# Float32 attention chunks: 1/sum moved from the weights of the values to their output, and every remainder of the MLP weights taken on VectorE

## Chip, cores and metric

One core of one Trainium2 chip runs the whole program. The metric is the device time of one execution in microseconds; lower is better. Engines are TensorE (PE in the rows: matmuls; PEld: its weight loads), VectorE (DVE), ScalarE (ACT), GpSimd (POOL) and SyncE (SP, which issues the transfers).

## What is computed

Sliding-window attention with sink tokens, then a two-layer MLP on its output:

```python
B, H, S, D = 4, 8, 768, 64          # n_sink = 4, window = 128
scores = q @ k.T / sqrt(D)           # keep: sink columns, or 0 <= row - col < window
scores = where(keep, scores, -1e9);  scores -= max(scores)
a = exp(scores);  a = a / (sum(a) + 1e-9)
x = (a @ v), heads side by side      # 3072 tokens x 512
h = x @ w_in;  r = max(h, 0)         # 512 x 2048
out = (s * r * r + b) @ w_out        # 2048 x 512
```

All inputs and the output are float32.

## The kernel before

**Chunks.** The 3072 tokens are eight chunks of 384 rows (three blocks of 128), taken in `ORDER`; for each chunk the attention of eight heads is made first, as four pairs of heads, and then the MLP reads it. Chunks 0 and 1 lie at the start of their sequences and use class `Plain`, with float32 matmuls; chunks 2 to 7 use `attn_slots`, which splits operands in two fp32r halves. Chunk 0's attention runs by itself. While the MLP of chunk c runs on TensorE, the slots of the attention of chunk c + 1 are woven in between its steps (the last loop of `tile_kernel`).

**The MLP.** `moe_steps` goes through 16 slices f of the hidden layer. `l1(f)` makes `h` with twelve matmuls (L608), then r (L611, ScalarE), s r r (L614, VectorE), g and its remainder (L616 ScalarE, L617 VectorE). `l2(f)`, two steps later, adds nine matmuls into three output banks `po` (L628). x, g and the weights each are a pair: a value rounded to fp32r and a remainder in fp32r; three products of a pair with a pair are taken. In chunk 0 (where `before` is set) s r r is written back into the PSUM bank of `h`, so this bank is held until L617 has read it. The banks of `h`, of the scores `sc`, of `o` and, in chunk 1, of the transposes `tp` come from one pool of five, `psA`.

**The weights.** They stay in SBUF as pairs, and are made once, while chunk 0 is computed. `load_weight(f)` brings slice f (1 MB) into the place of slice f + 1 as 64-bit numbers read as pairs of 32-bit words; `make_weight` turns it into float32 and then into the pair. `make_weight(2f)` has two ScalarE steps (L217, L218), two VectorE steps (L219, L220) and an addition on GpSimd in pieces of 256 columns (`in_parts`, L206). `make_weight(2f + 1)` writes the rounded value over place f (L226, ScalarE), and the following `make_weight(2f + 2)` the remainder: for even f on VectorE in one instruction (L231), for odd f on GpSimd in pieces (again L206). Slices 0 to 12 are one tile of 1024 columns, 13 and 14 are two pieces of 512, and 15 is four of 256. Since the raw slice f lies in the place of slice f + 1, L226 of f + 1 waits for the remainder of f.

**`Plain`.** For each pair: `scores` (matmuls L510, mask and maximum L525, exponential with row sum L527), `norm` (sum + 1e-9, reciprocal, and six scales of the weights of the values by it, L538), `turned` in three parts (transposes L550, copied out of PSUM by L552), `values` (matmuls L561; the rounded x by L563 on ScalarE, its remainder by L564 on VectorE).

**Order.** The program's text gives priorities; a scheduler sets the order on each engine, so that an edit can move neighbours. Each engine then runs its list strictly in order.

The lines of the weights that the change touches:

```python
        f -= 1
        if j % 2 == 0 and f >= 0:
            for c, raw in enumerate(raws[f]):
                do = in_parts if f % 2 == 1 else nc.vector.tensor_tensor
                do(out=piece(f, c, 1), in0=raw[..., 0].bitcast(F32), in1=piece(f, c, 0).bitcast(F32), op=ALU.subtract)
```

Of the kernel before, what the change touches and what calls it, by code (L numbers as in the profile page):

```python
# [6 lines left out]
F32 = mybir.dt.float32  # L7
# [5 lines left out]
ALU = mybir.AluOpType  # L13
AX = mybir.AxisListType

P = 128
B, H, S, D = 4, 8, 768, 64
ORDER = ((0, 0), (1, 0), (0, 1), (1, 1), (2, 0), (2, 1), (3, 0), (3, 1))
NS = 8
BLK = 3  # L20
CH = BLK * P
# [12 lines left out]
RB, VB = 1, 2  # L34
# [7 lines left out]
def tile_kernel(ctx, tc, qT, kT, k0, v, vsk, n_sink, window, w, s, b, out):  # L42
    nc = tc.nc
# [5 lines left out]
    def ps(name):  # L49
        return psA.tile([P, 512], F32, tag="a", name=name)  # L50

    wk_cm = tc.tile_pool(name="wk", bufs=2)
    wk = wk_cm.__enter__()
# [8 lines left out]
    ident = identr.bitcast(F32)  # L62
# [105 lines left out]
    def place(f):  # L168
        return (const if f < NEARLY else late[0]).tile([P, 2, 2, DM], F32, tag=f"w{f}", name=f"w{f}")
# [15 lines left out]
    def scratch(f, j):  # L185

        if len(raws[f]) == 1:
            tag = f"w{NF - 2 + f % 2}"
            return (late[0] if late else first).tile([P, 2, DM], I32, tag=tag, name="wt", bufs=1)
        return wk.tile([P, DM], I32, tag="ot", name="wt")[:, :raws[f][j].shape[1]]  # L190

    def piece(f, j, t):

        n = len(raws[f])
        if n == 1:
            return weight[f][:, :, t, :]
        a = DM * 2 // n
        return weight[f][:, j * 2 // n, t, j * a % DM:j * a % DM + a]

    def in_parts(out, in0, in1, op):  # L200

        n = out.shape[-1]
        for c in range(out.shape[1] if len(out.shape) == 3 else 1):
            for a in range(0, n, PART):
                q = (slice(None),) + ((c,) if len(out.shape) == 3 else ()) + (slice(a, min(a + PART, n)),)
                nc.gpsimd.tensor_tensor(out=out[q], in0=in0[q], in1=in1[q], op=op)  # L206

    def make_weight(j):

        f = j // 2
        if j % 2 == 0 and f < NF:
            for i, raw in enumerate(raws[f]):
                lo, hi = raw[..., 0], raw[..., 1]
                t = scratch(f, i)
                nc.scalar.activation(lo, lo.bitcast(U32), AF.Copy, scale=2.0 ** -29)  # L217
                nc.scalar.mul(hi.bitcast(F32), hi.bitcast(F32), 2.0 ** -111)  # L218
                nc.vector.tensor_scalar(out=t, in0=hi, scalar1=3, scalar2=None, op0=ALU.logical_shift_left)  # L219
                nc.vector.scalar_tensor_tensor(out=hi, in0=hi, scalar=-0x80000000, in1=t,  # L220
                                               op0=ALU.bitwise_and, op1=ALU.bitwise_or)
                in_parts(lo, hi, lo, ALU.add)
        if j % 2 == 1:
            weight[f] = place(f).bitcast(F32R)
            for c, raw in enumerate(raws[f]):
                nc.scalar.copy(piece(f, c, 0), raw[..., 1].bitcast(F32))  # L226
        f -= 1
        if j % 2 == 0 and f >= 0:
            for c, raw in enumerate(raws[f]):
                do = in_parts if f % 2 == 1 else nc.vector.tensor_tensor  # L230
                do(out=piece(f, c, 1), in0=raw[..., 0].bitcast(F32), in1=piece(f, c, 0).bitcast(F32), op=ALU.subtract)  # L231
            raws.pop(f)


# [227 lines left out]
    class Plain:  # L462
# [66 lines left out]
        def norm(self, pr):  # L529

            pp = self.pairs[pr]
            nc.vector.tensor_scalar(out=pp.z[:, 1], in0=pp.z[:, 0], scalar1=1e-9, scalar2=None, op0=ALU.add)
            nc.vector.reciprocal(out=pp.z[:, 0], in_=pp.z[:, 1])
            for i in range(BLK):
                c0, n = (0, P, 0)[i], (i + 1) * P
                for hh in range(2):
                    sm = pp.sm[2 * (i // 2) + hh][:, c0:c0 + n]
                    nc.vector.tensor_scalar(out=sm, in0=sm, scalar1=pp.z[:, 0, i, hh:hh + 1], scalar2=None, op0=ALU.mult)  # L538

        def turned(self, pr, part):  # L540

            pp = self.pairs[pr]
            if part == 0:
                pp.t = (wk if self.c else first).tile([P, 2, 2 * BLK, P], F32, tag="hl" if self.c else "tt0", name="tf", bufs=2)
            tp = (ps if self.c else po_bank)("tp")
            pos = (((0, 0), (2, 2)), ((1, 0), (1, 1)), ((2, 0), (2, 1)))[part]
            for hh in range(2):
                for j, (i, kb) in enumerate(pos):
                    c0 = (0, P, 0)[i] + kb * P
                    nc.tensor.transpose(tp[:, (2 * hh + j) * P:(2 * hh + j + 1) * P], pp.sm[2 * (i // 2) + hh][:, c0:c0 + P], ident)  # L550
            out = pp.t[:, :, part:part + (6 if part == 0 else 3):(5 if part == 0 else 2)]
            nc.scalar.copy(out, tp.rearrange("p (h k c) -> p h k c", h=2, c=P))  # L552

        def values(self, pr):
            pp = self.pairs.pop(pr)
            o = ps("o")
            for kb in range(BLK):
                for hh in range(2):
                    a = (0, 3, 5)[kb]
                    hs = slice(hh * D, (hh + 1) * D)  # L560
                    nc.tensor.matmul(o[hs, kb * P:CH], pp.v[:, kb, hh], pp.t[:, hh, a:a + BLK - kb].rearrange("p k c -> p (k c)"),  # L561
                                     start=(kb == 0), stop=(kb == BLK - 1))
            nc.scalar.copy(self.x[0][:, pr, :], o[:, :CH])  # L563
            nc.vector.tensor_tensor(out=self.x[1][:, pr, :], in0=o[:, :CH], in1=self.x[0][:, pr, :].bitcast(F32), op=ALU.subtract)  # L564

    def po_bank(name):
        return psO.tile([P, 512], F32, tag="po", name=name)
# [29 lines left out]
    def moe_steps(x, store, wk, before=None, last=False):  # L597
        g = {}
        po = [None] * BLK

        def l1(f):
            if before:
                before(f)
            h = ps("h")
            i = 0
            for cc in range(NCC):
                for wi, xi in ((0, 0), (0, 1), (1, 0)):
                    nc.tensor.matmul(h[:, :CH], weight[f][:, 0, wi, cc * P:(cc + 1) * P], x[xi][:, cc, :], start=(i == 0), stop=(i == 11))  # L608
                    i += 1
            r = wk.tile([P, CH], F32, tag="xsk" if before and f % 2 else "r", name="r", bufs=RB)  # L610
            nc.scalar.activation(r, h[:, :CH], AF.Relu, scale=1.0 / WUP)  # L611

            hr = h[:, :CH] if before else r
            nc.vector.scalar_tensor_tensor(out=hr, in0=h[:, :CH], scalar=sw_ap, in1=r, op0=ALU.mult, op1=ALU.mult)  # L614
            gg = wk.tile([P, 2, CH], F32R, tag="g", name="g", bufs=3)
            nc.scalar.activation(gg[:, 0, :], hr, AF.Identity, bias=b_ap, scale=1.0)  # L616
            nc.vector.scalar_tensor_tensor(out=gg[:, 1, :], in0=hr, scalar=b_ap, in1=gg[:, 0, :].bitcast(F32),  # L617
                                           op0=ALU.add, op1=ALU.subtract)
            g[f] = gg

        def l2(f):
            gg = g.pop(f)
            for tb in range(BLK):
                if f == 0:
                    po[tb] = psO.tile([P, DM], F32, tag="po", name="po")
                tsl = slice(tb * P, (tb + 1) * P)
                for i, (gi, wi) in enumerate(((0, 0), (0, 1), (1, 0))):
                    nc.tensor.matmul(po[tb], gg[:, gi, tsl], weight[f][:, 1, wi, :],  # L628
                                     start=(f == 0 and i == 0), stop=(f == NF - 1 and i == 2))
                if f == NF - 1:  # L630
                    own = dict(tag="kh", bufs=2) if tb == 2 else dict(tag="hl", bufs=HLB)
                    ot = wk.tile([P, DM], F32, name="ot", **(own if last else dict(tag="ot")))
                    nc.scalar.mul(ot, po[tb], 1.0 / WUP)
                    store(tb, ot)

        steps = []
        for f in range(NF + L2):
            if f < NF:
                steps.append(lambda f=f: l1(f))
            if f >= L2:  # L640
                steps.append(lambda f=f: l2(f - L2))
        return steps
# [101 lines left out]
    def before(f):  # L744
        weights(f + 2 + LOADS // 2, 2 * f + 5)
# [17 lines left out]
    k, slots = plain_slots(0)  # L763
# [19 lines left out]
    for c in range(NC_):  # L783
# [5 lines left out]
        if c + 1 < NC_:  # L789
            k, slots = plain_slots(1) if c == 0 else attn_slots(c + 1)  # L790
        i = 0
# [56 lines left out]
```

## Time and profile before

| | us |
|---|---|
| three runs | 730.23, 731.99, 732.29 |
| median | 731.99 |
| the profiled execution | 733.05 |
| its span, first to last instruction | 731.3 |
| chunk 0's attention, until the first L608 | 44.5 |
| first pass through the weights (MLP of chunk 0), until the next chunk's L608 | 44.5 to 150.8 |

Mean granted clock of TensorE over the span: 0.977 of full speed. The trace gives for each instruction its engine, line, operands, start and duration, and what ended the idle time before it. "x12" stands for twelve merged instructions; each float32 matmul of L510 and L561 is recorded as two. Durations of neighbours on an engine overlap by some tenths of a microsecond, so that a sum of single durations is a little more than the busy time.

### The profile page before, as it was taken

The numbers are of one execution on the slowest core, as the hardware profiler recorded it, in microseconds if no ns is written. First come the engines' busy times: TensorE is split into PE (matmuls) and PEld (weight loads), VectorE is DVE, ScalarE is ACT, GpSimd is POOL, SyncE is SP. The second block draws the span as 40 slices with busy tenths as digits, with TensorE's granted clock in tenths as the row PEclk, the third lists the DMA queues.
The fourth block names the chain that finished last, engine by engine and source line by source line (L and its number), as shares of the span: only waits on it lengthen the run. The fifth ranks groups of instructions, "written<-read, shape, count | busy, mean of one in ns | idle before, by whom it ended". The sixth has DMA issues, their size and how long they took to land.

```text
span 731.3 us, 11917 instructions
## 1 busy us (share of the span) xinstructions
PE 700.8 (96%) x3812; PEld 617.5 (84%) x3812; DVE 508.2 (69%) x1202; ACT 473.5 (65%) x1157; POOL 410.8 (56%) x703
## 2 busy tenths in 40 slices
PE   7599898999999999999999999999999999999996
PEld 4267666889988999899998999899999999989895
DVE  6969988548985788657786588847787589743331
ACT  6978877467774687656784677747775577633222
POOL 2556886348892588716674488915765389810000
PEclk8889988999999999999999999999999999999999
DMA  7845031131210212111111222111111212000001
GB/s 289 333 173 216 12 137 37 52 103 48 89 56 24 90 56 63 34 62 54 45 58 49 75 70 63 45 51 51 57 52 56 72 42 69 3 19 26 0 1 48
DMA packets 27381, 52.62 MB, mean 72 GB/s; under 512 B 3504, under 2 KB 15536, under 8 KB 25392
## 3 DMA queue, kind: packets, MB, share of 16 engines
q1 hardware_dynamic: 27312, 51.79, 21.3%
q8 instruction: 32, 0.52, 0.3%
q14 instruction: 37, 0.30, 0.1%
HBM read 45.49 MB, written 6.29 MB: 71 GB/s over the span
## 4 chain that ended last, share of the span: by engine, by line
PE 78%; DVE 9%; POOL 7%; ACT 3%; issue 2%; DMA 0%; SPq 0%; POOLq 0%; ACTq 0%; DVEq 0%
PE h L608 32%; PE po L628 32%; POOL w L206 4%; PE o L383 3%; PE sc L309 2%; PE sc L310 2%; PE sc L330 2%; DVE w L220 1%; PE tp L550 1%; PE o L561 1%; DVE smf L538 1%; DVE wt L219 1%; PE o L375 1%; POOL hl L346 1%; POOL kl L290 1%
## 5 line engine op out<-in xcount | busy, mean ns | idle before, releaser
L608 PE MATMUL h<-x,w 128*128 128x384 f32 x1536 | 297.7, 343 | 6.7 <-ACT tf L552 3.4
L628 PE MATMUL po<-w,g 128*128 128x512 f32 x1152 | 299.1, 405 | 0.0
L608 PEld LDWEIGHTS h<-x,w 128*128 128x128 f32 x1536 | 266.4, 189 | 13.1 <-ACT tf L552 3.8
L628 PEld LDWEIGHTS po<-w,g 128*128 128x128 f32 x1152 | 211.9, 191 | 45.6 <-issue 2.1
L614 DVE SCALAR_TENSOR_TENSOR r<-h,sb,r 128x384 f32<-128x384 f32 x112 | 68.9, 615 | 78.8 <-ACT r L611 77.7
L611 ACT ACTIVATE r<-h 128x384 f32<-128x384 f32 x128 | 62.6, 489 | 91.8 <-PE h L608 82.6
L617 DVE SCALAR_TENSOR_TENSOR g<-r,sb,g 128x384 fp32r<-128x384 f32 x112 | 91.1, 814 | 31.1 <-ACT g L616 29.6
L346 POOL TENSOR_TENSOR hl<-two,hl 128x256 fp32r<-128x256 f32 x128 | 102.3, 800 | 15.5 <-ACT hl L345 12.9
L323 POOL TENSOR_TENSOR sm<-sm 128x128 f32<-128x128 f32 x128 | 67.3, 526 | 60.9 <-ACT sm L320 59.1
L320 ACT ACTIVATE sm<-sm,negm 128x264 f32<-128x264 f32 (+1 forms) x144 | 72.1, 501 | 28.6 <-DVE negm L314 27.3
L616 ACT ACTIVATE g<-r,sb 128x384 fp32r<-128x384 f32 x112 | 69.1, 617 | 22.7 <-DVE r L614 22.0
L290 POOL TENSOR_TENSOR kl<-kraw,kh 128x528 fp32r<-128x528 f32 (+1 forms) x48 | 60.3, 1257 | 19.1 <-ACT kh L288 18.8
L206 POOL TENSOR_TENSOR w<-w 128x256 int32<-128x256 int32 x60 | 45.0, 780 | 40.3 <-DVE w L220 32.0
L345 ACT CAST hl<-two 128x256 fp32r<-128x256 f32 x128 | 50.5, 395 | 25.8 <-DVE two L343 25.5
L343 DVE TENSOR_TENSOR two<-sc,split 128x256 f32<-128x256 f32 x128 | 53.1, 417 | 5.8 <-POOL hl L346 5.5
L324 POOL COPY psk<-sm 128x24 f32<-128x24 f32 x144 | 35.5, 246 | 17.1 <-ACT sm L320 17.0
L383 PE MATMUL o<-hl,vv 128*128 128x256 f32 (+1 forms) x256 | 44.3, 275 | 0.0
L383 PEld LDWEIGHTS o<-hl,vv 128*128 128x128 f32 x256 | 39.6, 188 | 3.2
L289 DVE TENSOR_TENSOR qs<-qraw,qs 64x384 fp32r<-64x384 f32 x48 | 39.6, 825 | 3.7 <-ACT qs L285 1.9
L314 DVE CUSTOM_DVE_ANT_0 sm<-sc,m_all 128x264 f32<-128x264 f32 x64 | 27.3, 426 | 21.2 <-PE sc L310 19.2
L314 DVE CUSTOM_DVE_ANT_0 sm<-sc,msk 128x264 f32<-128x264 f32 (+1 forms) x80 | 32.0, 400 | 14.1 <-PE sc L310 13.4
L309 PE MATMUL sc<-kh,qs 128*128 128x264 f32 (+1 forms) x144 | 41.6, 291 | 0.0
(138 smaller groups left out, 960.4 us busy)
## 6 DMA issues: line engine op xcount, KB each, us to landing
w<-in_w SPq DMA_DIRECT2D x15, 1024.0 KB, 8.8
kraw<-in_kT SPq DMA_DIRECT2D x32, 264.0 KB, 2.6
out<-ot SPq DMA_DIRECT2D x24, 256.0 KB, 2.0
qraw<-in_qT SPq DMA_DIRECT2D x24, 192.0 KB, 2.4
vraw<-in_v SPq DMA_DIRECT2D x16, 256.0 KB, 2.8
kraw<-in_kT SPq DMA_DIRECT2D x16, 200.0 KB, 2.5
vsraw<-in_vsk SPq DMA_DIRECT2D x24, 64.0 KB, 2.1
vraw<-in_v SPq DMA_DIRECT2D x8, 192.0 KB, 2.4
```

What stands on the lines that cost most here:

```text
L206: nc.gpsimd.tensor_tensor(out=out[q], in0=in0[q], in1=in1[q], op=op)
L290: nc.gpsimd.tensor_tensor(out=hd.kl[:, :kw], in0=hd.k[:, :kw], in1=hd.kh[:, :kw].bitcast(F32), op=ALU.subtract)
L320: nc.scalar.activation(sm[:, :n], sm[:, :n], AF.Exp, bias=negm[:, uu], scale=-1.0, accum_out=pp.zz[:, i, hh:hh + 1])
L323: nc.gpsimd.tensor_tensor(out=sm[:, c1:c1 + P], in0=sm[:, p1:p1 + P], in1=sm[:, c1:c1 + P], op=ALU.add)
L346: nc.gpsimd.tensor_tensor(out=lo, in0=both, in1=hi.bitcast(F32), op=ALU.subtract)
L383: nc.tensor.matmul(hd.o[:, q0:q0 + n * P], hd.vv[:, kb, :], hd.hl[:, t, c0 * P:(c0 + n) * P], start=(hd.n == 0), stop=(i == BLK - 1 and kb ...
L608: nc.tensor.matmul(h[:, :CH], weight[f][:, 0, wi, cc * P:(cc + 1) * P], x[xi][:, cc, :], start=(i == 0), stop=(i == 11))
L611: nc.scalar.activation(r, h[:, :CH], AF.Relu, scale=1.0 / WUP)
L614: nc.vector.scalar_tensor_tensor(out=hr, in0=h[:, :CH], scalar=sw_ap, in1=r, op0=ALU.mult, op1=ALU.mult)
L616: nc.scalar.activation(gg[:, 0, :], hr, AF.Identity, bias=b_ap, scale=1.0)
L617: nc.vector.scalar_tensor_tensor(out=gg[:, 1, :], in0=hr, scalar=b_ap, in1=gg[:, 0, :].bitcast(F32), op0=ALU.add, op1=ALU.subtract)
L628: nc.tensor.matmul(po[tb], gg[:, gi, tsl], weight[f][:, 1, wi, :], start=(f == 0 and i == 0), stop=(f == NF - 1 and i == 2))
```

## The change

Four edits:
- `make_weight`: the remainder of odd f is taken on VectorE too, in whole pieces.
- `norm`: the six scales of each pair go; the reciprocal stays.
- `values`: six matmuls with the identity spread the reciprocals over the 64 output partitions of each head, into a bank `zb`. VectorE copies `o` to SBUF, multiplies it by `zb`, and the rounded x and its remainder are taken from the product. The product's tile has the tag "xsk" with one buffer; r in odd steps of chunk 0 had that tag, and has "r" now.
- `turned`: in chunk 0 the copy of part 1 moves from ScalarE to VectorE.

```diff
@@ make_weight
-                do = in_parts if f % 2 == 1 else nc.vector.tensor_tensor
-                do(out=piece(f, c, 1), in0=raw[..., 0].bitcast(F32), in1=piece(f, c, 0).bitcast(F32), op=ALU.subtract)
+                nc.vector.tensor_tensor(out=piece(f, c, 1), in0=raw[..., 0].bitcast(F32), in1=piece(f, c, 0).bitcast(F32), op=ALU.subtract)
@@ norm
-            for i in range(BLK):
-                c0, n = (0, P, 0)[i], (i + 1) * P
-                for hh in range(2):
-                    sm = pp.sm[2 * (i // 2) + hh][:, c0:c0 + n]
-                    nc.vector.tensor_scalar(out=sm, in0=sm, scalar1=pp.z[:, 0, i, hh:hh + 1], scalar2=None, op0=ALU.mult)
@@ turned
-            nc.scalar.copy(out, tp.rearrange("p (h k c) -> p h k c", h=2, c=P))
+            (nc.vector.tensor_copy if self.c == 0 and part == 1 else nc.scalar.copy)(out, tp.rearrange("p (h k c) -> p h k c", h=2, c=P))
@@ values
-            nc.scalar.copy(self.x[0][:, pr, :], o[:, :CH])
-            nc.vector.tensor_tensor(out=self.x[1][:, pr, :], in0=o[:, :CH], in1=self.x[0][:, pr, :].bitcast(F32), op=ALU.subtract)
+            zb = (ps if self.c else po_bank)("zb")
+            for i in range(BLK):
+                for hh in range(2):
+                    nc.tensor.matmul(zb[hh * D:(hh + 1) * D, i * P:(i + 1) * P], pp.z[:, 0, i, hh:hh + 1].to_broadcast([P, D]), ident,
+                                     start=True, stop=True)
+            y = wk.tile([P, CH], F32, tag="xsk", name="y0", bufs=1)
+            nc.vector.tensor_copy(y, o[:, :CH])
+            nc.vector.tensor_tensor(out=y, in0=zb[:, :CH], in1=y, op=ALU.mult)
+            nc.scalar.copy(self.x[0][:, pr, :], y)
+            nc.vector.tensor_tensor(out=self.x[1][:, pr, :], in0=y, in1=self.x[0][:, pr, :].bitcast(F32), op=ALU.subtract)
@@ l1
-            r = wk.tile([P, CH], F32, tag="xsk" if before and f % 2 else "r", name="r", bufs=RB)
+            r = wk.tile([P, CH], F32, tag="r", name="r", bufs=RB)
```

Line numbers shift: L614, L616 and L617 are L616, L618 and L619 after the change, L231 is L230, L608 is L610.

What the scheduler makes of it on GpSimd, at the weights f = 10 to 13 (the number in a tile's name is only its serial number; `w_824<-w_824` is the addition, `w_1070<-w_824,w_1070` the remainder, both L206). Before:

```order
L206 TENSOR_TENSOR w_749<-w_749 128x256 x4
L206 TENSOR_TENSOR w_824<-w_824 128x256 x4
L206 TENSOR_TENSOR w_1070<-w_824,w_1070 128x256 x4
L206 TENSOR_TENSOR w_895<-w_895 128x256 x4
L206 TENSOR_TENSOR w_1085<-w_1085 128x256 x2
L206 TENSOR_TENSOR w_1209<-w_1085,w_1209 128x256 x2
L206 TENSOR_TENSOR w_1085<-w_1085 128x256 x2
L206 TENSOR_TENSOR w_1209<-w_1085,w_1209 128x256 x2
```

Now:

```order
L206 TENSOR_TENSOR w_708<-w_708 128x256 x4
L206 TENSOR_TENSOR w_750<-w_750 128x256 x4
L206 TENSOR_TENSOR w_816<-w_816 128x256 x4
L206 TENSOR_TENSOR w_887<-w_887 128x256 x4
L206 TENSOR_TENSOR w_1075<-w_1075 128x256 x4
```

The remainders are gone from this list; only the additions are left.

On VectorE, at the weight f = 12 (`wt` and `w` in L219 and L220 are its two steps). Before:

```order
L220 SCALAR_TENSOR_TENSOR w_895<-w_895,wt 128x1024
L532 TENSOR_SCALAR zf<-zf 128x6
L533 RECIPROCAL zf<-zf 128x6
L538 TENSOR_SCALAR smf<-smf,zf 128x128 x2
L538 TENSOR_SCALAR smf<-smf,zf 128x256 x2
L538 TENSOR_SCALAR smf<-smf,zf 128x384
L538 TENSOR_SCALAR psk_96<-psk_96,zf 128x384
L231 TENSOR_TENSOR w_1134<-w_895,w_1134 128x2x512
L614 SCALAR_TENSOR_TENSOR h<-h,sb,r 128x384
L617 SCALAR_TENSOR_TENSOR g<-h,sb,g 128x384
```

Now:

```order
L220 SCALAR_TENSOR_TENSOR w_887<-w_887,wt 128x1024
L616 SCALAR_TENSOR_TENSOR h<-h,sb,r 128x384
L563 COPY y_1120<-o 128x384
L230 TENSOR_TENSOR w_1134<-w_887,w_1134 128x2x512
L619 SCALAR_TENSOR_TENSOR g<-h,sb,g 128x384
L564 TENSOR_TENSOR y_1120<-zb,y_1120 128x384
L566 TENSOR_TENSOR x_1_497<-y_1120,x_1_496 128x384
L219 TENSOR_SCALAR wt<-w_1075 128x512
```

The six scales are gone; the remainder, which reads what GpSimd adds after L220, now stands three places behind L220, with L619 behind it, and the copy and the product of the values have come in.

On TensorE, at a pair of values in chunk 1. Now:

```order
L555 MATMUL o<-tf,vf 64x384 x2
L555 MATMUL o<-tf,vf 64x256 x2
L555 MATMUL o<-tf,vf 64x128 x2
L560 MATMUL zb<-identr,zf 64x128 x6
L630 MATMUL po<-w_875,g 128x512 x9
```

The six matmuls of `zb` stand between the values and the next nine of `po`; the rest of the list keeps its sequence there, and from the MLP of chunk 1 on it is the same as before.

## Rows read from the trace of the kernel before

**Rows 1.** The page, part 4: chain that ended last, shares by line.

```profile
PE h L608 32%; PE po L628 32%; POOL w L206 4%; PE o L383 3%; PE sc L309 2%; PE sc L310 2%; PE sc L330 2%; DVE w L220 1%; PE tp L550 1%; PE o L561 1%; DVE smf L538 1%; DVE wt L219 1%; PE o L375 1%; POOL hl L346 1%; POOL kl L290 1%
```

**Rows 2.** Windows by stage: start:end, length, busy by engine (count), PEclk, DMA share, GB/s.

```profile
5.00:44.50 39.50, 27.08 (x149) 16.19 (x147) 33.42 (x119) 31.84 (x75) 13.95 (x21) 0.78 0.71 282
44.50:93.00 48.50, 43.60 (x226) 34.20 (x224) 44.10 (x85) 40.63 (x75) 36.92 (x44) 1.00 0.39 151
93.00:124.00 31.00, 27.75 (x119) 20.81 (x120) 25.15 (x49) 24.22 (x52) 22.57 (x29) 0.83 0.29 103
124.00:151.00 27.00, 27.00 (x141) 22.48 (x140) 14.81 (x30) 13.56 (x30) 9.00 (x13) 0.94 0.15 45
151.00:731.00 580.00, 571.54 (x3174) 522.34 (x3172) 389.77 (x917) 361.59 (x926) 325.69 (x584) 1.00 0.17 51
```

**Rows 3.** Waits of TensorE, 0 to 140 us: us, times, longest.

```profile
PE tp L550 <- DVE sm L538: 7.4, 2, 5.2
...
PE sc L510 <- DVE g L617: 3.4, 3, 2.2
PE h L608 <- ACT tf L552: 3.4, 2, 2.2
PE h L608 <- DVE g L617: 1.4, 1, 1.4
```

**Rows 4.** Waits of all engines, 0 to 135 us.

```profile
ACT w L226 <- POOL w L206: 9.0, 5, 3.7
...
DVE w L231 <- POOL w L206: 5.0, 3, 3.3
```

**Rows 5.** Timeline: start, us, engine, line, tiles [idle before <-releaser].

```profile
105.35 2.35 PE L608 MATMUL h<-x,w 128*128 128x384 f32 x12
...
115.68 0.91 PE L510 MATMUL sc<-kf,qf 64*128 64x384 f32 x2 [0.88 <-DVE g L617]
...
119.93 1.93 POOL L206 TENSOR_TENSOR w<-w,w 128x256 fp32r<-128x256 f32 x2
...
121.83 2.32 POOL L206 TENSOR_TENSOR w<-w 128x256 int32<-128x256 int32 x4
121.90 0.66 ACT L226 CAST w<-w 128x512 fp32r<-128x512 f32 x1 [3.72 <-POOL w L206]
...
122.45 0.60 ACT L552 COPY tf<-tp 128x512 f32<-128x512 f32 x1
...
123.10 3.56 PE L608 MATMUL h<-x,w 128*128 128x384 f32 x12 [2.22 <-ACT tf L552]
```

**Rows 6.** Busy time of L538 alone, by stage.

```profile
5.00:44.50 39.50, 9.74 (x24) 0.78 0.71 282
44.50:151.00 106.50, 14.44 (x24) 0.94 0.30 110
```

**Rows 7.** Groups by line, 0 to 130 us: us busy, mean ns.

```profile
L206 POOL TENSOR_TENSOR w<-w 128x256 int32<-128x256 int32 x60 | 45.0, 780 | 40.3 <-DVE w L220 32.0 <-ACT w L218 8.3
L206 POOL TENSOR_TENSOR w<-w,w 128x256 fp32r<-128x256 f32 x28 | 27.9, 1025 | 2.7 <-ACT w L226 2.7
...
L231 DVE TENSOR_TENSOR w<-w,w 128x1024 fp32r<-128x1024 f32 x7 | 9.4, 1346 | 5.0 <-POOL w L206 5.0
...
L552 ACT COPY tf<-tp 128x512 f32<-128x512 f32 x21 | 12.0, 580 | 1.1 <-PE tp L550 0.9
```

**Rows 8.** Single lines, min/median/max ns.

```profile
L231 DVE TENSOR_TENSOR w<-w,w x9: 676/1214/1619, 29.3 to 131.5; 128x1024 fp32r<-128x1024 f32 x7, 128x512 fp32r<-128x512 f32 x2
...
L564 DVE TENSOR_TENSOR x<-o,x x8: 546/555/559, 19.1 to 149.2; 128x384 fp32r<-128x384 f32 x8
```

**Rows 9.** Timeline of TensorE at the last pair of chunk 1.

```profile
147.12 1.51 PE L561 MATMUL o<-tf,vf 128*64 128x384 f32 x12
148.56 2.36 PE L628 MATMUL po<-w,g 128*128 128x512 f32 x9
```

**Rows 10.** Timeline: end of chunk 0's attention.

```profile
46.56 0.55 DVE L564 TENSOR_TENSOR x<-o,x 128x384 fp32r<-128x384 f32 x1
```

## The prediction

> **What bounds the kernel now.** The chain that ended last is mostly two matmul lines of TensorE, L608 and L628, with GpSimd's L206 as the largest entry of another engine [rows 1]. The windows by stage show where that entry lies [rows 2]. From 151 us on TensorE is busy 571.5 of 580 us at full clock: nothing the other engines save there counts. Before that there are two stages with slack. In the attention of chunk 0 (5 to 44.5 us) TensorE works 27.1 of 39.5 us at a granted clock of 0.78, while VectorE is busy 33.4 and ScalarE 31.8. In the first pass through the weights (44.5 to 151 us) TensorE idles in short gaps and its clock falls: 0.83 from 93 to 124 us and 0.94 from 124 to 151, that is, part of the time at 1.2 instead of 2.4 GHz.
>
> The waits of TensorE name these gaps [rows 3]: 7.4 us for the scales of L538, all in the first stage; in the second 3.4 us and 1.4 us for L617 and 3.4 us for L552, 8.2 us in all. The waits of the others say who stands behind them [rows 4]: ScalarE's L226 waits 9.0 us for GpSimd, VectorE's L231 5.0 us. One place shows the whole chain [rows 5]: GpSimd subtracts a remainder until 121.86, ScalarE has idled 3.72 us in front of L226, which needs it, the copy L552 queued behind L226 runs at 122.45, and TensorE, idle 2.22 us for that copy, starts its matmuls at 123.10, at half clock: 3.56 us for the twelve, which took 2.35 at 105.35 us [rows 5].
>
> So the limit of the second stage is the making of weights and the queues it runs through. Its slack: 8.2 us idle, and for the clock 0.17 x 2 x 31 + 0.06 x 2 x 27 = 13.8 us at 1.2 GHz, of which 3.1 us (the 0.88 and 2.22 us gaps in it [rows 5]) are idle and counted already; the remaining 10.7 us of work would have taken 5.3 us less. Slack: 13.5 us of 106.5.
>
> **The change part by part.** *Scales out.* The 48 instructions of L538 go: 9.7 us of VectorE in the first stage, 14.4 us in the second [rows 6]. The transposes no longer wait for them; they wait for the exponentials alone.
>
> *Remainders to VectorE.* GpSimd loses 32 pieces at about 1.02 us [rows 7], an estimated 32 us; all but the four of f = 1, some 28 us, lie in the second stage. VectorE gains six of 1024 columns, two of 512 and four of 256. The wide one exists in the trace, 1.35 us on average, between 1.21 and 1.62 [rows 7, 8]; the small ones are bounded by 0.68 (the shortest of L231, which has 512 columns [rows 8]) and half of that. That is 1.35 in the first stage (f = 1), and 5 x 1.35 + 2 x 0.68 + 4 x 0.35 = 9.5 us in the second. The spread from 1.21 to 1.62 is what the rows show when GpSimd works beside it. The Trainium skill (GPSIMD Engine Reference, Key points) says why: GpSimd shares its SBUF interfaces with VectorE, and instructions with two SBUF inputs contend. By that rule, which speaks against moving a two-input subtract, every wide one would cost 1.62, and VectorE would pay 1.4 us more in the second stage. I keep 1.35, because GpSimd's own load there falls by these 28 of 68.5 us [rows 2].
>
> *Product behind the values.* Each of eight pairs adds a copy and a multiply of 384 columns that read PSUM. The nearest row is L564, of that size and also reading PSUM, 0.55 us [rows 8]: 1.1 us a pair, 4.4 us in each stage. The subtract is there before and after, and so is ScalarE's copy.
>
> *Copies.* In chunk 0 four copies of 512 columns leave ScalarE, 4 x 0.58 = 2.3 us [rows 7], for VectorE, taken at 0.65 each between 0.55 (L564) and 0.74 (L564 by columns): 2.6 us.
>
> *TensorE.* Six small matmuls a pair (zb), 768 columns. The nearest rows are the value matmuls, also float32 with 64-wide weights: 1536 columns in 1.44 us to the start of the next group, recorded as twelve [rows 9]. By columns that is 0.72 us a pair, by number of records 1.44, as each float32 matmul there shows as two. I take 0.72, since the form is the same: 2.9 us in the second stage; 5.8 is the upper end. In the first stage they lie in idle time. The Trainium skill (FP8 and Floating Point Precision, TensorE Precision Notes) says that true FP32 takes four passes through the array; by 4 x 768 columns at 2.4 GHz that would be an estimated 1.28 us a pair, 5.1 us, and the sum 2.2 us later. The row of the value matmuls is below what that rule gives for them (2.56 us), so the row decides.
>
> *One buffer for r.* Odd steps of chunk 0 lose their second one. ScalarE's order has the bias step L616 of one f ahead of the next L611, and L616 already waits for L614, the reader of r, so this costs nothing; if that order broke, a step would wait for one L614.
>
> *Behind the last pair* of chunk 1 nine matmuls of L628 (2.36 us [rows 9]) and nine of the next L608 come before its x is read. The longer way (copy, product, ScalarE's copy, subtract: some 2.1 us) fits; without that cover it would cost 1.1 us.
>
> The sum for VectorE: first stage -9.7 + 1.35 + 4.4 + 2.6 = -1.4 us; second -14.4 + 9.5 + 4.4 = -0.5, so its load stays at about 83.6 us there (84.1 before [rows 2]), in a better order: six scales in a row no longer stand in front of L614 and L617.
>
> *First stage.* The 7.4 us of waiting for the scales is the most that can go. But the queues of VectorE and ScalarE feed each other here through exponential, copy and product, and neither has much air [rows 2]; what they lose together is 1.4 + 2.3 = 3.7 us, while the last pair's way to its x gains a copy and a product, which at the start of the matmuls costs some tenths, since L564 ended it at 47.1 us [rows 10]. I take 3.5; the lower bound is a loss of 1 us (the longer way, 1.1, and nothing gained), the upper 7.4 gained.
>
> *Second stage.* All of the slack would bring TensorE to 106.5 - 13.5 + 2.9 = 95.9 us. VectorE at 83.6 us would then be busy 87% against 79% before, and ScalarE, unchanged at 78.4 us, 82%. What waits for GpSimd disappears, and with it the clock drop that follows such a gap; what remains is the delay of L617 behind other VectorE work. I leave a third of the slack, 4.1 us: 100 us, so 6.5 us gained. What is late next is VectorE.
>
> Sum against the profiled execution: 733.05 - 3.5 - 6.5 = 723.0 us. That execution was 1.06 us above the median of the three runs, so the median becomes about 722.0. A measurement of this kernel can tell about 0.3%, 2.2 us.
>
> **The rivals.**
> - *VectorE takes over as the limit.* For: 79% busy already, and L617 holds TensorE for 4.8 us [rows 3]. Against: its load doesn't grow. Then only the first stage gains: about 728.5. Chance 0.18.
> - *TensorE's floor.* All slack goes: 731.99 - 3.5 - 10.6 = 717.9. Chance 0.13. Against: the gaps at L617 are VectorE's own, and its load stays.
> - *Slower: the subtract blocks VectorE's queue.* It needs GpSimd's four additions, 2.3 to 3.1 us of work behind L220 (four in 2.32 us, 0.78 each on average [rows 5, 7]). For the last weights the new order puts only one product of L614 and one copy, 1.2 us or so, between L220 and the subtract; everything behind it, L617 above all, then waits. At 90% usable, eleven subtracts that wait 1.9 us each make (83.6 + 21) / 0.9 = 116 us, 10 us more than now: about 738. It turns slower from about 1.4 us a subtract. Against: most subtracts stand several instructions behind. Chance 0.10.
> - *No net change: PSUM banks.* Each pair of chunk 1 takes one bank more of a pool of five, whose release is what TensorE waits for at L617 (3.4 + 1.4 us [rows 3]). If these waits double and the clock still falls, the stage gains 3.4 - 4.8 - 2.9 = -4.3 and the first stage gives 3.5: about 732.8. Chance 0.08.
>
> **How the numbers follow.** The forecast has 0.51. Faster by over 0.3%, below 729.8: forecast, floor and most of the first rival, 0.80; same 0.08, from the rest of it and the banks; slower 0.12. The range 716 to 730 takes in the floor with a larger first stage (up to 5 us) and the first rival, and leaves out the two last cases.
>
> **What would show it.** Right: no wait for GpSimd at L226; GpSimd's L206 only 64 times and no more in the chain; the second stage near 100 us and the clock above 0.95 from 93 us on; the first matmul of L608 near 41 us (lines by the numbers of before). Wrong: the new subtract idling VectorE for GpSimd by over 1 us each; zb far above 0.72 us a pair; TensorE waiting longer for bank release; a first stage as long as before; or any change after the first pass.

## The result, and the profile after

The changed kernel takes **715.58 us** (median of five runs, 715.33 to 716.13) against 731.99 (five runs, 730.23 to 733.08): a ratio of 0.9778, 95% interval 0.9765 to 0.979. Faster, as forecast, but by 16.4 us where 10.0 were forecast: it lies just below the range. The profiled execution took 715.33 us with a span of 713.6.

The change by stage, from windows of the trace after, cut at its first L610 (36.20 us) and at the first product of the next chunk (133.18 us); columns as in [rows 2]:

```profile
5.00:36.20 31.20, 24.63 (x197) 15.41 (x195) 26.62 (x104) 27.86 (x70) 7.29 (x13) 1.00 0.90 357
36.20:93.00 56.80, 55.11 (x304) 43.63 (x304) 51.97 (x100) 53.35 (x101) 34.46 (x40) 1.00 0.42 155
93.00:133.18 40.18, 37.79 (x230) 30.77 (x227) 31.02 (x63) 25.44 (x56) 15.19 (x20) 1.00 0.23 73
133.18:713.00 579.82, 571.66 (x3175) 522.49 (x3173) 390.06 (x917) 361.08 (x927) 325.71 (x584) 1.00 0.17 51
```

The first stage, up to the first L610, ends 8.3 us earlier (44.52 before). The second takes 36.20 to 133.18, 97.0 us, where it took 44.52 to 150.76, 106.2: 9.3 us less. From there on nothing moved: 571.66 us of TensorE work, 571.54 before [rows 2]. The granted clock is 1.00 in every window. TensorE idles 4.1 us of the second stage; up to 93 us ScalarE is busy 53.35 of 56.80 us, fuller than before, and VectorE 51.97, as full as before (91%).

The waits of all engines up to 135 us (engine, line, releaser: us in total, times, longest), against [rows 3, 4]:

```profile
ACT w L226 <- DVE w L230: 6.2, 2, 5.9
...
DVE w L230 <- POOL w L206: 4.6, 4, 1.6
...
ACT w L217 <- DMA w<-in_w: 3.9, 2, 3.3
...
PE h L610 <- DVE w L230: 2.6, 2, 1.6
PE tp L544 <- ACT tf L546: 2.2, 2, 1.5
...
PE tp L544 <- DVE tf L546: 2.1, 1, 2.1
```

The two waits of L544 lie in the first stage. In the second TensorE waits 2.6 us for L230, 0.8 for L524 (`PE h L610 <- DVE negm L524: 0.8, 1, 0.8`) and twice 0.3 us in front of L610. The 7.4 us for the scales and the waits for L617 are gone, and so is every wait of L226 for GpSimd. The chain on the page, against [rows 1], no longer has L206:

```profile
PE h L610 32%; PE po L630 32%; PE o L382 3%; PE sc L308 2%; PE sc L309 2%; PE sc L329 2%; DVE w L230 1%; DMA w<-in_w 1%; DVE w L220 1%; PE o L374 1%; DVE wt L219 1%; POOL hl L345 1%; POOL kl L289 1%; PE os L406 1%; PE ts L397 1%
```

The groups of 0 to 130 us (us busy, mean ns | idle before), against [rows 7]:

```profile
L206 POOL TENSOR_TENSOR w<-w 128x256 int32<-128x256 int32 x60 | 48.6, 840 | 54.3 <-DVE zf L532 15.1 <-ACT r L613 9.5 <-DVE w L220 8.2
...
L230 DVE TENSOR_TENSOR w<-w,w 128x1024 fp32r<-128x1024 f32 x13 | 16.7, 1281 | 4.7 <-POOL w L206 4.6
...
L564 DVE TENSOR_TENSOR y<-zb,y 128x384 f32<-128x384 f32 x7 | 3.8, 549 | 0.0
L563 DVE COPY y<-o 128x384 f32<-128x384 f32 x7 | 3.8, 543 | 1.7 <-PE o L555 1.7
```

And TensorE at the last pair of chunk 1, against [rows 9]:

```profile
128.88 1.52 PE L555 MATMUL o<-tf,vf 128*64 128x384 f32 x12
130.22 0.83 PE L560 MATMUL zb<-identr,zf 128*64 128x128 f32 x12
130.98 2.37 PE L630 MATMUL po<-w,g 128*128 128x512 f32 x9
```

The prices held: the wide remainder 1.28 us (taken: 1.35), copy and product 0.54 and 0.55 (0.55 each), zb 0.76 us to the next start (0.72). So the miss lies in what the engines wait for and in TensorE's clock, not in what the new instructions cost.

### The profile page after: what moved, and what is told of

Read it like the earlier page. It is cut to its first block, busy times and chain, and to the rows that moved or that the text cites. A ratio compares the mean times of both kernels' runs of the same rounds, so it can differ in the third digit from the quotient of the medians.

```text
span 713.6 us, 12060 instructions
## 1 busy us (share of the span) xinstructions
PE 693.0 (97%) x3908; PEld 613.8 (86%) x3908; DVE 500.6 (70%) x1186; ACT 469.4 (66%) x1153; POOL 385.3 (54%) x671
## 4 chain that ended last, share of the span: by engine, by line
PE 76%; DVE 6%; ACT 3%; POOL 2%; issue 1%; DMA 1%; POOLq 0%; ACTq 0%; DVEq 0%
PE h L610 32%; PE po L630 32%; PE o L382 3%; PE sc L308 2%; PE sc L309 2%; PE sc L329 2%; DVE w L230 1%; DMA w<-in_w 1%; DVE w L220 1%; PE o L374 1%; DVE wt L219 1%; POOL hl L345 1%; POOL kl L289 1%; PE os L406 1%; PE ts L397 1%
## 5 line engine op out<-in xcount | busy, mean ns | idle before, releaser
L610 PE MATMUL h<-x,w 128*128 128x384 f32 x1536 | 297.6, 342 | 6.0 <-DVE w L230 2.6
L630 PE MATMUL po<-w,g 128*128 128x512 f32 x1152 | 295.9, 402 | 0.0
L610 PEld LDWEIGHTS h<-x,w 128*128 128x128 f32 x1536 | 264.8, 188 | 14.3 <-DVE w L230 3.3
L630 PEld LDWEIGHTS po<-w,g 128*128 128x128 f32 x1152 | 209.8, 189 | 43.7 <-issue 1.6
L616 DVE SCALAR_TENSOR_TENSOR r<-h,sb,r 128x384 f32<-128x384 f32 x112 | 68.9, 615 | 78.8 <-ACT r L613 77.9
L619 DVE SCALAR_TENSOR_TENSOR g<-r,sb,g 128x384 fp32r<-128x384 f32 x112 | 91.5, 817 | 31.3 <-ACT g L618 29.7
L618 ACT ACTIVATE g<-r,sb 128x384 fp32r<-128x384 f32 x112 | 69.1, 617 | 22.7 <-DVE r L616 21.9
L206 POOL TENSOR_TENSOR w<-w 128x256 int32<-128x256 int32 x60 | 48.6, 840 | 54.3 <-DVE zf L532 15.1
```

## The experiments

For each kernel that ran the table gives the median and, from the windows of its trace, where the first layer-one product (the first matmul of `l1`) starts, how long the second stage takes from there to the first such product of the next chunk, TensorE's busy time in it, and the difference, which is its idle time. After that stage each of them needs 580 us more. Names are explained below.

| kernel | median | first product | stage | busy | idle |
|---|---|---|---|---|---|
| before | 731.99 | 44.52 | 106.2 | 98.1 | 8.2 |
| after | 715.58 | 36.20 | 97.0 | 92.9 | 4.1 |
| e1: remainders alone | 721.19 | 42.86 | 96.1 | 91.4 | 4.7 |
| e2: output product alone | 732.38 | 38.48 | 111.1 | 98.9 | 12.1 |
| e3: both, copies on ScalarE | 716.27 | 39.54 | 94.6 | 93.0 | 1.6 |
| e6: e3, chunk 0 scales | 718.14 | 44.12 | 93.1 | 91.8 | 1.2 |
| e7: e3, chunk 1 scales | 723.68 | 38.50 | 103.3 | 94.2 | 9.1 |
| e4: before, filled behind the reciprocals | 749.59 | 59.02 | 108.2 | 97.4 | 10.8 |
| e4b: before, filled | 732.47 | 44.03 | 107.2 | 96.0 | 11.2 |
| e11: after, remainder 1 on GpSimd | 720.91 | 36.39 | 102.6 | 96.0 | 6.6 |
| e8: after, remainders 1, 3, 5, 7 on GpSimd | 726.59 | 36.82 | 107.1 | 98.4 | 8.7 |
| e9: after, remainders 9, 11, 13, 15 on GpSimd | 724.06 | 37.66 | 104.4 | 95.2 | 9.2 |
| e5: after, spreading twice | 718.82 | 42.01 | 95.0 | 93.8 | 1.2 |
| e10: after, chunk 1's L566 on GpSimd | 716.28 | 37.06 | 97.8 | 94.0 | 3.8 |
| e13: after, spreading from GpSimd's copy | 713.46 | 36.80 | 94.6 | 93.3 | 1.3 |
| e12: e13 with wide products | 712.53 | 36.11 | 94.1 | 92.9 | 1.3 |

Each edit also lets the scheduler move neighbours; a difference of one or two microseconds between two rows may be that. The mean granted clock of the second stage is 0.94 to 0.97 in the kernels that take remainders on GpSimd (before, e2, e4, e4b, e8, e9, e11) and 0.98 to 1.00 in all others.

**The parts of the change, one by one.** e1 is the kernel before with one edit:

```diff
-                do = in_parts if f % 2 == 1 else nc.vector.tensor_tensor
-                do(out=piece(f, c, 1), in0=raw[..., 0].bitcast(F32), in1=piece(f, c, 0).bitcast(F32), op=ALU.subtract)
+                nc.vector.tensor_tensor(out=piece(f, c, 1), in0=raw[..., 0].bitcast(F32), in1=piece(f, c, 0).bitcast(F32), op=ALU.subtract)
```

> The kernel before with one part of the change: all remainders of the weights on VectorE; the scales stay. Theory A (the second stage's gain comes from the remainders leaving GpSimd, since ScalarE's rounding then no longer waits 9.0 us for it): the first stage stays near 44.5 us with the clock near 0.78, the second stage falls from 106.3 to 97 to 99 us, total 723 to 725 us. Theory B (it comes from the 48 scales leaving VectorE's queue, and the remainders only fit because those left): the second stage stays at 104 us or more, total 730 us or more, VectorE busy over 0.95 of the window from 44 to 93 us.

e2 is the changed kernel with that edit and the move of the copies undone.

> The changed kernel with the odd remainders on GpSimd as before and all copies of the transposes on ScalarE: 1/sum on the output is the only part left. If the first stage's 8.3 us are the scales' gaps and the clock that fell in them, the first layer-one product starts at 36 to 38 us with a clock of 0.95 or more up to there. Theory A for the second stage: it stays at 104 to 106 us, with waits of ScalarE for GpSimd, total 723 to 725 us. Theory B: it falls to 97 to 99 us too, total 717 to 719 us.

Measured: e1 721.19 (ratio 0.9852, 0.9837 to 0.9867), e2 732.38 (1.0016, 1.0002 to 1.0031). Theory A got the sign of e1 and was outdone by its size. Neither had e2 right: the first stage did end 6.0 us earlier there, and the second grew by 4.8. The remainders alone are worth 10.8 us, the output product alone nothing. In e2 (waits up to 150 us) the two engines that wait for GpSimd now do so for longer than in [rows 4], 9.0 and 5.0:

```profile
ACT w L226 <- POOL w L206: 15.5, 7, 4.8
...
DVE w L231 <- POOL w L206: 13.3, 4, 4.2
```

So with the remainders on GpSimd the making of weights sets the time, and an earlier start of the second stage only waits longer for it.

**The copies.** e3 is the changed kernel with this line as before:

```diff
-            (nc.vector.tensor_copy if self.c == 0 and part == 1 else nc.scalar.copy)(out, tp.rearrange("p (h k c) -> p h k c", h=2, c=P))
+            nc.scalar.copy(out, tp.rearrange("p (h k c) -> p h k c", h=2, c=P))
```

> The changed kernel with every copy of the transposes on ScalarE. If the move of chunk 0's second copies to VectorE is a small part, 715.6 to 717 us and a first stage within 1 us of 36.2. Rival: it is ScalarE's queue that decides the first stage once the scales are gone, then the first layer-one product starts at 38 us or later and the total is 717.5 to 719 us.

716.27 us (five runs, 715.24 to 716.56; after: 715.33 to 716.13). The first product starts at 39.54, 3.3 us later than with the move, as the rival had it, and yet the total is where the first theory put it, the same within what can be told: the second stage takes up 2.4 of the 3.3.

**Chunk 0's scales against chunk 1's.** Both kernels are e3 with the scales kept in one chunk:

```diff
+            if self.c == 0:      # e7: == 1
+                for i in range(BLK):
...
+                        nc.vector.tensor_scalar(out=sm, in0=sm, scalar1=pp.z[:, 0, i, hh:hh + 1], scalar2=None, op0=ALU.mult)
...
+            if self.c == 0:      # e7: == 1
+                nc.scalar.copy(self.x[0][:, pr, :], o[:, :CH])
+                nc.vector.tensor_tensor(out=self.x[1][:, pr, :], in0=o[:, :CH], in1=self.x[0][:, pr, :].bitcast(F32), op=ALU.subtract)
+                return
```

> The kernel with all copies on ScalarE and all remainders on VectorE, but chunk 0 still scales its weights of the attention (chunk 1 multiplies its output). It lies between the kernel with remainders alone (721.2 us, stage ends 138.94) and the one without any scale (716.3, stage ends 134.16). Theory C (one chain of weight preparation through VectorE's queue ends the second stage, so every scale that leaves that queue counts about the same wherever it is): chunk 0's 24 scales are worth 2 to 3 of the 5 us, total 718 to 719 us. Theory D (first stage decides: the start of the first layer-one product moves one to one): with chunk 0's scales back the first layer-one product is at 42 to 43 us and the total at 719.5 to 721 us.

> The mirror of the last: chunk 0 multiplies its output, chunk 1 still scales its weights of the attention; copies on ScalarE, remainders on VectorE. Theory C: chunk 1's 24 scales are worth 2 to 3 of the 5 us, total 718 to 719 us. Theory D: first layer-one product near 39.5 us as without scales, total 716 to 717.5 us.

e6 718.14 us (ratio 0.9803, 0.9786 to 0.9819), e7 723.68 (0.9885, 0.9869 to 0.9902). Theory D falls: with chunk 0's scales back the first product stands at 44.12, as in the kernel before, and 13.9 of the 16.4 us are there all the same. Windows of e6, the second up to 0.2 us before the stage's end:

```profile
5.00:44.12 39.12, 27.72 (x150) 16.58 (x148) 33.38 (x120) 32.68 (x76) 9.73 (x17) 0.78 0.72 285
44.12:137.00 92.88, 91.64 (x530) 74.42 (x529) 81.82 (x157) 76.13 (x154) 49.95 (x56) 1.00 0.36 126
```

TensorE then idles 1.2 us. That the later start does it, by leaving the weights more lead, is argued and not shown: e12 and e13 below idle as little with an early start. Theory C's sizes nearly fit chunk 0 in e6 (1.9 us from e6 to e3, at the edge of what can be told, where 2 to 3 were expected) but not e7: chunk 1's scales cost 7.4 us when put back alone, and 3.1 from e1 to e6. In e7 TensorE idles 9.1 us, 4.8 of it for VectorE's remainders. Why it is 2.5 us slower than e1, with fewer scales, was not settled.

**Is it the clock?** Before, the first stage ran at 0.78 [rows 2], after at 1.00, which suggests that the gaps slowed TensorE itself. e4 put products into the gaps of the kernel before:

```diff
+            if self.c == 0:
+                wq = po_bank("wq")
+                for i in (*range(BLK),) * 3:
+                    for hh in range(2):
+                        nc.tensor.matmul(wq[hh * D:(hh + 1) * D, i * P:(i + 1) * P], pp.z[:, 0, i, hh:hh + 1].to_broadcast([P, D]), ident, start=True, stop=True)
```

> The kernel before with 18 unused 64x128 products per pair of chunk 0, put between the reciprocal and the transposes, so that TensorE works while VectorE scales; all waits for the scales stay, the output is the same. If the clock is the larger half of the first stage's gain (gaps lower it, full activity holds it): granted clock up to the first layer-one product 0.92 or more, value products of chunk 0 back from 2.4 to 2.8 us to about 1.5 us, first layer-one product at 39 to 42 us, total 727 to 730 us. If only VectorE's and ScalarE's queues set the first stage, as the forecast had it: first layer-one product at 44 to 46 us, total 731 to 734 us.

749.59 us: a failed experiment. The fillers need the reciprocals, TensorE's list is in order, and it waited 11.9 us for them in three places before it could go on. e4b does it without a new dependence:

```diff
+            if self.c == 0 and part == 0:
+                for _ in range(10):
+                    nc.tensor.matmul(tp, warm[:, :P], warm, start=True, stop=True)
```

> The kernel before with ten unused 128x512 products per pair of chunk 0, written into the bank that the transposes then overwrite, so no further bank is held and nothing waits for the reciprocals; the output is the same. If the clock of the first stage carries a large part of the change's gain: granted clock from 20 to 44 us 0.95 or more, value products of chunk 0 near 1.5 us instead of 2.5 to 2.8, first layer-one product at 40 to 42 us, total 728 to 730 us. If the clock there is a by-product and the weights' preparation sets the end of the second stage: the clock rises all the same, the total stays at 731 to 733 us.

732.47 us (ratio 1.0, 0.9991 to 1.001). The mean clock of the first stage rose to 0.91:

```profile
5.00:44.03 39.03, 32.82 (x188) 17.37 (x189) 32.38 (x119) 31.73 (x75) 14.10 (x21) 0.91 0.72 286
```

and the first product came 0.5 us earlier. VectorE (32.4 of 39.0 us) and ScalarE (31.7) are nearly as full as before, which would account for so small a gain. What the step from 0.91 to 1.00 is worth this does not show: one of chunk 0's groups of value products still took 2.08 us, where two took 1.51 and 1.52. But in e6 the clock is 0.78 and the first product at 44.12, as before, and 13.9 us are gained all the same; for the total the clock of the first stage counts for little.

**What a remainder on GpSimd costs.** Three kernels are the changed one with some odd weights back on GpSimd:

```diff
-                nc.vector.tensor_tensor(out=piece(f, c, 1), in0=raw[..., 0].bitcast(F32), in1=piece(f, c, 0).bitcast(F32), op=ALU.subtract)
+                (in_parts if f in (1, 3, 5, 7) else nc.vector.tensor_tensor)(out=piece(f, c, 1), in0=raw[..., 0].bitcast(F32), in1=piece(f, c, 0).bitcast(F32), op=ALU.subtract)
```

> The changed kernel with the remainders of weights 1, 3, 5 and 7 back on GpSimd, where one takes four parts of about 1.03 us, 4.1 us in all, against 1.2 us on VectorE. Theory L (a remainder on GpSimd costs by its length, wherever it stands, because the preparation of weights is one chain): four of eight cost about half of what all cost with the scales gone (16 us between 716.3 and 732.4), total 721 to 724 us. Theory V (up to 76 us VectorE is the full engine, so early remainders are better placed on GpSimd): 714 to 716.5 us.

> The changed kernel with the remainders of weights 9, 11, 13 and 15 back on GpSimd. Theory L: 721 to 724 us as with the early ones. Theory V: the late ones are what the change is worth, 723 to 728 us, with TensorE waiting for weights between 90 and 120 us.

> The changed kernel with the remainder of weight 1 alone back on GpSimd, which is idle for 25 of the 35 us before 40 us. If VectorE's 1.2 us near 30 us are worth more than GpSimd's 4.1: 714 to 715.3 us. If its length counts even there: 716 to 718.5 us.

(1, 3, 5, 7) give 726.59 us, (9, 11, 13, 15) 724.06, (1,) alone 720.91 (six runs, 716.71 to 725.06, so that its cost is known to some 2 us only). Theory V falls: the early ones cost 11.0 us, the late ones 8.5, and the first by itself 5.3, though GpSimd is idle most of the time there. Theory L had the sign and was too low: 721 to 724 for both groups and at most 718.5 for the first alone; nor do the costs add up, since 11.0 and 8.5 are more than the 16.1 of all eight (e2 against e3). The timeline of e11 shows the way:

```profile
35.03 5.59 POOL L206 TENSOR_TENSOR w<-w,w 128x256 fp32r<-128x256 f32 x4
...
40.65 1.14 ACT L226 CAST w<-w 128x1024 fp32r<-128x1024 f32 x1 [3.22 <-POOL w L206]
...
43.76 0.49 ACT L565 CAST x<-y 128x384 fp32r<-128x384 f32 x1
...
44.28 0.74 DVE L566 TENSOR_TENSOR x<-y,x 128x384 fp32r<-128x384 f32 x1 [3.04 <-ACT x L565]
...
44.30 1.01 PE L610 MATMUL h<-x,w 128*128 128x384 f32 x2 [3.60 <-ACT x L565]
```

GpSimd takes 5.59 us for four parts; the next rounding, L226, may not overwrite what they read, so ScalarE stands for 3.22 us; behind it in ScalarE's list are two steps of the next weight and the rounded x of the last pair (43.76 us; 40.17 in the trace after); TensorE waits 3.60 us for that; e8 has the same wait, 3.6 us. It is the mechanism of [rows 5], at the other end of the stage. Over the whole second stage of e11 TensorE idles 2.5 us more than after the change and is busy 3.0 us longer, at a mean granted clock of 0.90 from 36 to 90 us, where it was 1.00. By these windows about half of the price is waiting and half is slower work.

**What is left.** e5 and e10 are the changed kernel with each spreading product twice (`for i in (*range(BLK), *range(BLK))`), and with chunk 1's L566 on GpSimd.

> The changed kernel with each spreading product done twice, the second over the first; the output is the same. 8 pairs x 0.75 us = 6.0 us more of TensorE. If TensorE is now what bounds the second stage, chunk 1's four pairs show: 718 to 719 us. If the queues of VectorE and ScalarE still bound it, 715.5 to 716.5 us.

> The changed kernel with chunk 1's four subtractions for the second part of x on GpSimd: 4 x 0.5 us leave VectorE. If VectorE's queue still holds TensorE up between 36 and 118 us (idle there about 4 us): 714 to 715.2 us. If not, or if a longer subtraction on GpSimd delays its additions: 715.3 to 717 us.

e5 takes 718.82 us: 3.2 more, the number forecast for TensorE as the bound, but not for that reason. By its parts it comes from a first product at 42.01 in place of 36.20, of which the second stage (95.0 us) took back 2.0; TensorE's busy time in that stage grew by 0.9 us only. e10 takes 716.28 (714.15 to 717.67): no difference that can be told.

Last, e12 halves the columns of the spreading products, and e13 takes the width back but leaves GpSimd's copy in. The edit of e12, which also puts the copy into the one buffer of the product's tile:

```diff
+            zx = wk.tile([P, CH], F32, tag="xsk", name="zx", bufs=1)
+            nc.gpsimd.tensor_copy(zx.rearrange("p (g d) -> p g d", d=D), pp.z[:, 0].rearrange("p i h -> p (i h)").unsqueeze(2).to_broadcast([P, 2 * BLK, D]))
...
-                for hh in range(2):
-                    nc.tensor.matmul(zb[hh * D:(hh + 1) * D, i * P:(i + 1) * P], pp.z[:, 0, i, hh:hh + 1].to_broadcast([P, D]), ident, start=True, stop=True)
+                nc.tensor.matmul(zb[:, i * P:(i + 1) * P], zx[:, i * P:(i + 1) * P], ident, start=True, stop=True)
```

> The changed kernel with the spreading done by three 128x128 products a pair in place of six 64x128: GpSimd first copies each reciprocal over 64 columns. Half as many columns pass through TensorE (384 a pair in place of 768). If the products cost by columns passed (0.75 us a pair now, 0.37 then) and TensorE's own work bounds the second stage, chunk 1's four pairs give 1.5 us: 713.8 to 714.6 us. If the 64-wide products already run side by side, or if the queues bound the stage: 715.3 to 717 us, a little later where GpSimd's copy is waited for.

> As the last kernel, with GpSimd's copy of the reciprocals, but six 64x128 products a pair again, which read that copy. The three wide products took 0.69 us a pair to the next start and the six narrow ones 0.75, so if TensorE's time in them were the gain, little of the 3.05 us would be due to width. If the other order that GpSimd's copy and its longer path give is what pays: 712.3 to 713.5 us. If the width pays after all: 715 to 717 us.

e12 takes **712.53 us** (ratio 0.9727, 0.9714 to 0.974), 3.05 us below the changed kernel: the fastest of all. e13 takes 713.46 (713.38 to 714.43; ratio 0.9747, 0.9728 to 0.9766). So 2.1 of the 3.05 come with GpSimd's copy and what it moves; the 0.9 left for the width are less than these ratios can tell (their intervals overlap). The product itself hardly got shorter; the timeline of e12 (0.69 us to the next start, where the narrow ones took 0.76):

```profile
125.94 1.51 PE L557 MATMUL o<-tf,vf 128*64 128x384 f32 x12
127.38 0.94 PE L561 MATMUL zb<-identr,zx 128*128 128x128 f32 x6
128.07 2.34 PE L630 MATMUL po<-w,g 128*128 128x512 f32 x9
```

Both kernels start the second stage within 0.6 us of the changed one, and TensorE idles 1.3 us in it in place of 4.1. What does that, one of the moved neighbours or the waits that the shared buffer adds, was not tried apart.

## Why the prediction was right and wrong

**Right.** The sign; the stages named (all of the gain before the second chunk, none behind); the prices of the new instructions; no wait of L226 for GpSimd, L206 64 times, and out of the chain; a clock above 0.95 from 93 us on; and VectorE as what is late next (L230, 2.6 of TensorE's 4.1 us). The subtract waits for GpSimd four times, 1.6 us at most, 4.6 in all, so the rival with VectorE's queue blocked did not come; nor did longer waits for bank release: the second stage has one that can be such, 0.8 us for L524.

**Luck.** The 4.1 us left of the slack are also TensorE's measured idle time there, 4.1. But they were to be the delay of L617, and no such wait is left.

**The step that failed** is the sum "733.05 - 3.5 - 6.5": both of its terms were too small. The first stage gained 8.3 us where 3.5 were taken and 7.4 were the upper bound; the second gained 9.3 where 6.5 were taken. By the experiments the second term carries the change: the remainders alone (e1) give 10.8 us. Two things were missed in it:

- *The work of TensorE.* All of the slack was to leave 95.9 us with the new products. After the change TensorE is busy 92.9 us with them, 4 x 0.75 = 3.0 of which are theirs: 89.9 us for the old work, which took 98.1 before. That is 8.2 us less, where 5.3 had been put down for the low clock. Windows of the trace before (columns as in [rows 2]) show an error in the 5.3:

```profile
93.20:100.00 6.80, 6.80 (x17) 4.75 (x18) 5.14 (x6) 5.98 (x8) 6.80 (x8) 0.50 0.56 212
114.80:115.68 0.88, 0.00 (x0) 0.00 (x0) 0.85 (x3) 0.88 (x3) 0.88 (x2) 1.00 0.00 0
117.10:120.50 3.40, 3.40 (x11) 2.60 (x9) 3.40 (x5) 1.08 (x3) 3.40 (x5) 0.51 0.43 137
120.88:123.10 2.22, 0.00 (x0) 0.00 (x1) 1.34 (x6) 1.20 (x3) 2.22 (x5) 1.00 0.00 0
123.95:127.25 3.30, 3.30 (x14) 3.20 (x12) 3.30 (x10) 2.88 (x9) 2.17 (x5) 0.50 0.00 0
```

The gaps of 0.88 and 2.22 us were subtracted from the time at 1.2 GHz, but the granted clock in them is 1.00, and where it is 0.50 TensorE is busy throughout. So half of all 13.8 us, 6.9, is the clock's price. What is left of the 8.2 is not the clock; the scores' products (L510) are part of it, busy 11.5 us before and 8.7 after.

- *What a remainder holds up.* It was costed as load: 28 us off GpSimd, 9.5 onto VectorE. But an engine's list is in order, and a part on GpSimd is paid for by whoever stands behind the rounding that waits for it. One alone costs some 5 us (e11). [rows 5] showed that very chain, and the sum used it only for gaps and clock.

**The term of the first stage** was too small as a length and wrong as a part of a sum. The first product moved by 8.3 us: 1.7 with the remainders (before to e1), 3.3 by the scales (e1 to e3) and 3.3 by the copies (e3 to after); the "upper 7.4" was a wait for scales only and left out the rest. But that start is worth far less than its length: nothing while GpSimd makes the remainders (e2), 1.9 us of the 4.6 that chunk 0's scales move it once it does not (e6 to e3), and less than can be told for the copies' 3.3. The two terms were added as if each stage had its own time; but weights made in the first stage are used in the second, and by these runs an earlier start is mostly paid back there. Taken along one path (before, e1, e6, e3, after) the 16.4 us are: remainders 10.8, chunk 1's scales 3.1, chunk 0's 1.9, copies 0.7 (the last two at or below what can be told). This split holds for that path only: by way of e7 chunk 0's scales would cost 2.5 us and chunk 1's give 7.4.

**The rivals.** "TensorE's floor" (717.9) is nearest (715.58), and for its reason in part: in e3, e6, e12 and e13 TensorE idles 1.2 to 1.6 us of the stage. The changed kernel itself still leaves 4.1. Its argument against, that the gaps at L617 are VectorE's own and would stay, was wrong: no such wait is left, though VectorE's load is as forecast (83.0 us in the stage; 83.6 forecast).

## What to carry to other kernels

When a chain of preparation runs through several in-order engines, cost a slow step in it by what stands behind the instruction that waits for it on each engine, not by the load it takes off its own. Before adding up the gains of two stages, ask whether the earlier one hands the later one something besides its start; if so, an earlier start may buy only an earlier wait, and the parts have to be tried in both orders. And price a low granted clock by what the engine does at it: 6.9 us here in the second stage, where TensorE was busy in all of that time; nothing that can be told in the first, where 0.91 in place of 0.78 left the total as it was (e4b).

## What the runs showed that was not expected

- The same four parts of a remainder on GpSimd take very different times: in e11, with VectorE and ScalarE full, 5.59 us; its additions of 128x256 lie between 0.60 and 1.70 us in that trace. VectorE's subtract of 1024 columns ranges from 1.21 to 1.62 us there, and that of 512 columns from 0.68 to 1.82. The Trainium skill (GPSIMD Engine Reference, Key points) says that GpSimd shares its SBUF interfaces with VectorE, and that VectorE instructions with two SBUF inputs contend with it. The spread agrees with that; no run here tried it apart.
- A float32 product of full width (128 outputs, 128 columns) takes 0.23 us (0.69 / 3, in e12); the two of half width that give the same take 0.25 together (0.76 / 3). The Trainium skill (FP8 and Floating Point Precision, TensorE Precision Notes) gives four passes for true FP32, an estimated 0.21 us for 128 columns at 2.4 GHz. The wide rows agree with it. The narrow ones come to half of that each because two run at a time: in the trace after, their records start two by two, 7 ns apart (130.222 and 130.229 us, then 130.331 and 130.338), while those of the wide ones in e12 start singly, 0.11 us apart from the second on. So e12's case of products that already run side by side was the true one, and its halved columns could save next to nothing.
- Unneeded work on TensorE raised its granted clock from 0.78 to 0.91 at no cost and no gain in the total (e4b), and a dependence too many made a similar filling cost 17.6 us (e4).
